# Attention with a relative bias, then routed experts: score products on 64 rows, two groups a visit, earlier transposes, a shorter way to the bias table

## The chip, the cores and the metric

The kernel runs on one core of a Trainium2 chip. The metric is the device time of the kernel in microseconds (us), lower is better. Before the change it is 409.79 us, the median of three runs (408.8 to 410.69).

A core has five engines that work side by side and meet at semaphores: TensorE (PE, matmul; PEld is its weight load), VectorE (DVE), ScalarE (ACT), GpSimd (POOL) and SyncE (SP, which here only starts transfers). An engine carries out its own instructions in order.

## The reference

```
scores = q @ k^T / sqrt(64)                      # 8 batches, 8 heads, 576 positions, head width 64
bias   = bias_table[bucket(|i - j|)]             # 32 buckets; one bucket for all |i - j| >= 128
attn   = exp(scores + bias) / sum                # softmax over the keys
x      = attn @ v                                # 4608 tokens x 512
e      = hash(token_id) mod 8                    # one expert for each token
out    = relu(x @ w1[e]) @ w2[e]                 # 512 -> 1024 -> 512
```

Inputs and output are float32; both kernels multiply in float16 and add up in float32.

## The kernel before

**Stages.** The first stage is the attention; it leaves its rows in DRAM, each at a place in the list of its expert (`xperm`). The second stage takes the experts one after the other: 640 places each, two layers, and a scatter into the output. Its code is the same in both kernels.

**Pairs and groups.** Attention goes over 32 pairs: a batch and two neighbouring heads. A pair has 512 positions in four key tiles of 128, and 64 positions left over (the rest). It is worked in five groups, 0 to 3 for the key tiles and 4 for the rest. A group is a PSUM slot of 128 keys x 2 heads x 512 queries. There are three such slots (`ps`, two banks each), taken in turn.

**One group.** `products(n, g)` multiplies keys by queries; `scores(n, g)` adds the bias by multiplying a flipped identity with a strip of the bias table (`bias`, so a matmul of 384 columns a head), and then ACT takes the exponential of the whole slot into `att`. The bias lies only near the diagonal; the far value is taken off beforehand, since the softmax is blind to a constant. `behind(n, g)` follows with nine of the 45 steps of AV (attention times values, `av_steps`), which runs seven groups behind the scores. A pair's AV fills two accumulators: `aux0` (27 steps) and `aux1` (18 steps). DVE empties them with a reciprocal and a product.

**Both heads in one product.** The keys of a pair lie as 128 rows, 64 of each head. In `kz` each head's 64 rows stand beside 64 rows of zeros, so that a matmul over 128 rows gives the scores of one head; a group has two such matmuls of 512 columns.

**Transposes.** `transpose_qk(n + 1)`, eight matmuls into `pqk`, is placed behind the AV steps of group 3 of pair n. `pqk` shares a bank with `aux1`. DVE then copies `pqk` to `kz` (two copies of 64 rows) and to `qt` (one). The products of pair n+1 come one group later.

**The rest.** Once a batch, `transpose_rest` and `rest_rest` prepare the scores among the 64 leftover positions of all four pairs; `rest_rest` puts them into `prr`, which shares a bank with `aux0`, and ACT takes their exponential into `rr`.

**Order.** The order in each engine is that in which the code is written. `pair_start(n)` puts the loads of pair n+4 on SP's queue and the casts of pair n+2 to float16 on POOL; in some pairs also fills, dispatches (indirect writes of finished rows) and expert weights. A transfer started by SP or ACT may have to wait for an earlier one that used the same completion semaphore.

**The start.** A one-hot matrix (`ohsb`, 32 x 1152) times the table gives the bias for every distance; ACT writes it to DRAM (`t_f`), from where shifted strips are read back: `btb` for the key tiles (heads 0 and 1 first, the other six later) and `btr` for the rest. All of these transfers stand on ACT's queue.

Of the kernel before, what the change touches and what calls it, by code (L numbers as in the profile page):

```python
# [11 lines left out]
F32 = mybir.dt.float32  # L12
F16 = mybir.dt.float16
I32 = mybir.dt.int32
AF = mybir.ActivationFunctionType
# [16 lines left out]
def kernel(  # L32
# [20 lines left out]
    P = 128  # L53
# [19 lines left out]
    GL = 3 * P  # L73
    OH_np = np.zeros((NB, 3, GL), dtype=np.float32)
    for dl in range(3):
        for y in range(GL):
            r = 2 * (y - GL // 2 + 1) + dl - 1
            OH_np[bucket[min(abs(r), S - 1)], dl, y] += 1.0
            OH_np[last, dl, y] -= 1.0
    OH_np = OH_np.reshape(NB, 3 * GL)  # L80
    I128_np = np.zeros((P, 3, P), dtype=np.float16)
# [67 lines left out]
    with tc.tile_pool(name="at", bufs=1) as at, tc.tile_pool(  # L149
# [11 lines left out]
        x_all = at.tile([P, B, NIT, XW], F16, name="x_all")  # L161
        kz = [at.tile([P, 2, KT * P], F16, name=f"kz{i}") for i in range(3)]
        va = [at.tile([P, 2 * KT, VP], F16, name=f"va{i}") for i in range(3)]
# [6 lines left out]
        btb = at.tile([P, H, 3, WB], F16, name="btb")  # L170
        btr = at.tile([P, NPAIR, 2, D + RU], F16, name="btr")
        te = at.tile([P, NGT], I32, name="te")
# [194 lines left out]
        def transpose_qk(n, eng=None):  # L367
            pqk = aux(1, [P, 2, KT * P], F16, "pqk")
            for i, src in enumerate((kh, qh)):
                for t in range(KT):  # L370
                    T, c = t // 2, t % 2
                    o = P * t if i == 0 else NT * P * c + P * T
                    nc.tensor.transpose(  # L373
                        out=pqk[:, i, o : o + P],
                        in_=src[n][:, t, :, :].rearrange("p h d -> p (h d)"),
                        identity=ident[:, :],
                    )
            for hh in range(2):
# [4 lines left out]
            kts[n] = kz[n % 3]  # L383
            qt = at.tile([P, KT * P], F16, name="qt", bufs=2)
            nc.vector.tensor_copy(out=qt[:, :], in_=pqk[:, 1, :])  # L385
            qts[n] = qt
# [31 lines left out]
        def rest_rest(b):  # L418
            prr = aux(0, [P, NPAIR, RC], F32, "prr")
            for m in range(NPAIR):  # L420
                nc.tensor.matmul(
                    out=prr[:, m, :], lhsT=kzr[b % 2][:, m, :],
                    rhs=qtr[b % 2][:, m, :], start=(m == 0), stop=True,
                    skip_group_check=True,
                )
            bias(
                prr[:, :, :].rearrange("p m (o u) -> p m o u", o=2),
                btr[:, :, :, D : D + RU], 2,
            )
# [15 lines left out]
        def products(n, g):  # L445
# [6 lines left out]
            for t in tiles:  # L452
                for hh in range(2):
                    lhsT = kt[:, hh, P * t : P * t + P]
                    rhs = qt[:, :] if g < KT else qtr[b % 2][:, m, :]
                    o = 0 if g < KT else RC * t
                    nc.tensor.matmul(  # L457
                        out=ps[:, hh, o : o + rhs.shape[1]], lhsT=lhsT,
                        rhs=rhs, start=(g < KT or t == 0), stop=True,
                        skip_group_check=True,  # L460
                    )

        def scores(n, g):
# [3 lines left out]
            for hh in range(2):  # L467
# [16 lines left out]
                for t in range(KT - 2, KT):  # L484
# [5 lines left out]
                    )  # L490
                bias(ps[:, hh, 512 - D :], btr[:, m, hh, :D], 2)
            nc.scalar.activation(  # L492
# [79 lines left out]
        nc.scalar.dma_start(out=tbl[:, :], in_=bias_table)  # L572
        ohsb = at.tile([NB, 3 * GL], F32, name="ohsb")
        nc.scalar.dma_start(out=ohsb[:, :], in_=OH_d.ap())
# [3 lines left out]

        def z_init(i):
            nc.gpsimd.memset(kz[i][D:P, 0, :], 0.0)  # L580
            nc.gpsimd.memset(kz[i][:D, 1, :], 0.0)

        z_init(0)
        cast_qk(0, nc.vector, nc.vector)
        bps = [slot("bps") for _ in range(2)]
        ebsb = at.tile([H, 3, GL], F16, name="ebsb")
        for i in range(3):
            nc.tensor.matmul(
                out=bps[i // 2][:H, i % 2, :GL], lhsT=tbl[:, :],
                rhs=ohsb[:, GL * i : GL * i + GL],  # L590
            )
        for i in range(2):
            w = 2 - i
            nc.scalar.activation(
                out=ebsb[:, 2 * i : 2 * i + w, :],
                in_=bps[i][:H, :w, :GL], func=AF.Copy, bias=0.0,
                scale=1.0 / scale,
            )
        nc.scalar.dma_start(
# [3 lines left out]

        def load_band(h0, h1):
            nc.scalar.dma_start(
                out=btb[:, h0:h1, :, :].rearrange("p h a w -> p (h a) w"),
# [5 lines left out]

        load_band(0, 2)
        for hh in range(2):
            for c in range(2):
                for o in range(2):
                    r0 = D * hh + RU * c
                    nc.scalar.dma_start(
                        out=btr[r0 : r0 + RU, :, o, :],
                        in_=bass.AP(  # L620
                            F_d.ap().tensor,
                            (3 * hh + o - c + 1) * GL + P - RU,
                            [[1, RU], [6 * GL, NPAIR], [1, D + RU]],
                        ),
                    )
        transpose_qk(0)
        load(0, "v")
        load(1, "qk")
        for i in range(2):
# [10 lines left out]
        for i in range(3):  # L640
            nc.gpsimd.memset(va[i][:, :, D : D + 1], 1.0)
        cast_v(0)
        load_rest(0, "v")
        load(1, "v")
        cast_qk(1)
        z_init(1)
        cast_vrest(0)
        load_band(2, H)
        load(2)
        load(3)  # L650
        z_init(2)
        nc.sync.dma_start(out=msk[:, :], in_=MSK_d.ap())
# [31 lines left out]
        def pair_start(n):  # L684
# [30 lines left out]
        def behind(n, g):  # L715
# [242 lines left out]
```

## Time and profile before

| | us |
|---|---|
| median of three runs | 409.79 |
| the profiled execution, device time | 408.63 |
| its span, first to last instruction | 406.7 |
| busy: PE, ACT, POOL, DVE | 351.2, 211.4, 167.1, 136.2 |
| ACT exponentials of the scores (160) | 161.7 |
| PE products of key tiles (256) | 78.9 |
| PE bias matmuls of key tiles (256) | 64.6 |
| PE AV matmuls of 65 columns (1280) | 64.6 |

Between the span and the device time lie 1.9 us. Busy times of PE are no sums of work: a matmul counts from its first column to its modelled end, and the next one starts before that end. What a matmul costs PE is read from one start to the next. In the rows, `x8` after a form is the number of instructions in a merged row, and a bracket at the end names the idle time before it and what ended it.

### The profile page before, as it was taken

How to read it: one execution, taken by the hardware profiler on the slowest of the kernel's cores; microseconds unless marked ns; L12 is line 12 of the kernel's file. 1: busy time of each engine (PE TensorE's matmuls, PEld its weight loads, DVE VectorE, ACT ScalarE, POOL GpSimd, SP SyncE). 2: the span in 40 equal slices, each digit the busy share in tenths (PEclk: the TensorE clock that was granted, in tenths of full speed). 3: DMA queues.
4: the chain of work that ended last, by engine and by line, in shares of the span. 5: the costliest groups of instructions: out<-in, count | busy, mean ns of one | idle time of the engine just before them, and what ended most of it. 6: DMA issues, size and time to landing. Idle time of an engine off the chain costs nothing.

```text
span 406.7 us, 9256 instructions
## 1 busy us (share of the span) xinstructions
PE 351.2 (86%) x3792; PEld 229.0 (56%) x3792; DVE 136.2 (33%) x339; ACT 211.4 (52%) x235; POOL 167.1 (41%) x248
## 2 busy tenths in 40 slices
PE   4278999899999999999999807999999999999990
PEld 1035666566666666666666605665657575656650
DVE  1211346544434444344443401323140413223220
ACT  2046877687787877878778601322415051423320
POOL 3713225242576666583846040152333515151331
PEclk9998999999999999999999966999999999999997
DMA  6795967969685755997984025399999999995211
GB/s 172 192 244 147 266 134 215 272 189 269 196 237 169 206 176 134 249 186 212 235 174 94 10 77 175 53 204 159 258 161 266 201 193 261 160 264 115 89 70 61
DMA packets 95107, 72.66 MB, mean 179 GB/s; under 512 B 16295, under 2 KB 86183, under 8 KB 95056
## 3 DMA queue, kind: packets, MB, share of 16 engines
q0 software_dynamic: 17664, 30.96, 36.1%
q1 hardware_dynamic: 72880, 38.98, 35.1%
q10 hardware_dynamic: 4512, 2.04, 2.0%
q8 instruction: 32, 0.52, 0.5%
q14 instruction: 19, 0.16, 0.1%
HBM read 69.27 MB, written 21.03 MB: 222 GB/s over the span
## 4 chain that ended last, share of the span: by engine, by line
PE 71%; DVE 10%; DMA 8%; ACT 4%; issue 2%; SPq 2%; POOL 1%; POOLq 0%; ACTq 0%; DVEq 0%
PE hps L788 17%; PE ops L806 17%; PE ps L457 13%; PE ps L438 9%; PE px L523 8%; DVE kz L379 6%; ACT att L492 3%; PE pqk L373 3%; DVE qt L385 3%; PE xps L767 2%; DMA btb<-t_f 2%; DMA qf<-in_q_dram 2%; DMA xpn<-t_xperm 1%; DMA btr<-t_f 1%; SPq L188 1%
## 5 line engine op out<-in xcount | busy, mean ns | idle before, releaser
L492 ACT ACTIVATE att<-ps 128x1024 f16<-128x1024 f32 x160 | 161.7, 1023 | 58.6 <-PE ps L438 41.8
L794 ACT ACTIVATE h<-hps 128x640 f16<-128x640 f32 x64 | 45.0, 704 | 112.9 <-PE hps L788 112.9
L457 PE MATMUL ps<-qt,kz 128*128 128x512 f16 x256 | 78.9, 391 | 15.4 <-DVE qt L385 13.9
L438 PE MATMUL ps<-btb,idents 128*128 128x384 f16 (+1 forms) x384 | 78.2, 288 | 8.8 <-DMA btb<-t_f 8.8
L806 PE MATMUL ops<-w2t,h 128*128 128x512 f16 x320 | 72.7, 379 | 0.0
L788 PE MATMUL hps<-xpt,w1t 128*128 128x320 f16 x512 | 72.1, 301 | 0.1
L523 PEld LDWEIGHTS <-att 128*128 128x128 f16 x1408 | 61.0, 98 | 18.6 <-ACT rr L430 3.5
L523 PE MATMUL px<-va,att 128*128 128x65 f16 x1280 | 64.6, 193 | 1.2 <-DVE rcp L532 0.4
L438 PEld LDWEIGHTS <-idents 128*128 128x128 f16 x456 | 39.7, 100 | 42.0 <-issue 12.4
L814 POOL DMA_INDIRECT out_dram<-ok,xpn x40 | 39.2, 980 | 57.4 <-DVE ok L813 51.3
L788 PEld LDWEIGHTS <-w1t 128*128 128x128 f16 x512 | 50.4, 99 | 21.2 <-issue 0.3
L379 DVE COPY kz<-pqk 64x512 f16<-64x512 f16 x64 | 27.0, 422 | 77.6 <-PE pqk L373 76.6
L806 PEld LDWEIGHTS <-h 128*128 128x128 f16 x320 | 30.8, 98 | 33.4
L548 POOL DMA_INDIRECT t_xperm<-x_all,ds x40 | 39.4, 985 | 21.9 <-DVE rcp L532 11.3
L813 DVE COPY ok<-ops 128x512 f32<-128x512 f32 x40 | 27.7, 692 | 47.0 <-PE ops L806 47.0
L457 PEld LDWEIGHTS <-kz 128*128 128x128 f16 x512 | 28.2, 99 | 22.2 <-DVE qt L385 18.7
L771 DVE COPY xpt<-xps 128x640 f16<-128x640 f16 x32 | 15.0, 488 | 74.2 <-PE xps L767 59.7
L226 POOL CAST qh<-qf 128x512 f16<-128x512 f32 x31 | 19.0, 613 | 42.9 <-PE pqk L373 25.5
L533 DVE TENSOR_TENSOR x_all<-px,rcp 128x384 f16<-128x384 f32 x64 | 31.4, 491 | 2.2
L234 POOL CAST va<-vf 128x512 f16<-128x512 f32 x32 | 20.0, 624 | 28.5 <-PE px L523 15.7
L132 POOL DMA_DIRECT2D w1t<-in_moe_w_dram x8 | 6.5, 810 | 52.0 <-PE xps L767 51.9
L532 DVE RECIPROCAL rcp<-px 128x6 f32<-128x6 f32 x64 | 11.7, 183 | 42.4 <-PE px L523 42.4
(72 smaller groups left out, 243.0 us busy)
## 6 DMA issues: line engine op xcount, KB each, us to landing
kf<-in_k_dram SPq DMA_DIRECT2D x64, 128.0 KB
qf<-in_q_dram SPq DMA_DIRECT2D x64, 128.0 KB
vf<-in_v_dram SPq DMA_DIRECT2D x64, 128.0 KB
w1t<-in_moe_w_dram POOLq DMA_DIRECT2D x8, 1024.0 KB, 9.6
w2t<-in_moe_w_dram POOLq DMA_DIRECT2D x8, 1024.0 KB, 10.4
t_xperm<-zx SPq DMA_DIRECT2D x10, 514.0 KB
xpn<-t_xperm SPq DMA_DIRECT2D x8, 642.5 KB
btb<-t_f ACTq DMA_DIRECT2D x1, 1152.0 KB
```

The lines of the kernel that those rows point to most:

```text
L379: nc.vector.tensor_copy(out=kz[n % 3][D * hh : D * hh + D, hh, :], in_=pqk[D * hh : D * hh + D, 0, :],)
L438: nc.tensor.matmul(out=out, lhsT=idents[:, which, :], rhs=rhs, start=False, stop=True, skip_group_check=True,)
L457: nc.tensor.matmul(out=ps[:, hh, o : o + rhs.shape[1]], lhsT=lhsT, rhs=rhs, start=(g < KT or t == 0), stop=True, skip_group_check=True,)
L492: nc.scalar.activation(out=att[:, g, :, :], in_=ps[:, :, :], func=AF.Exp, bias=0.0, scale=scale,)
L523: nc.tensor.matmul(out=po, lhsT=lhsT, rhs=rhs, start=(i == 0), stop=(i == len(todo) - 1), skip_group_check=True,)
L533: nc.vector.tensor_tensor(out=x_all[:, b, its[0] : its[0] + ni, :DM].rearrange("p t (m h d) -> p t m h d", h=2, m=NPAIR)[:, :, m, :, :], i ...
L548: sc_in = nc.gpsimd.indirect_dma_start(out=xperm_d.ap()[:, :], out_offset=bass.IndirectOffsetOnAxis(ap=ds2[:, B * t + b : B * t + b + 1], ...
L788: nc.tensor.matmul(out=hps[:, nr, :NR], lhsT=w1h[:, kt, ts(ft, P)], rhs=xt[e][:, kt, ts(nr, NR)], start=(kt == 0), stop=(kt == NPT - 1),)
L794: nc.scalar.activation(out=h1[:, ft, :].rearrange("p (r n) -> p r n", r=NRC), in_=hps[:, :, :NR], func=AF.Relu, bias=0.0, scale=1.0,)
L806: nc.tensor.matmul(out=ops[:, :], lhsT=h1[:, ft, ts(kc, P)], rhs=w2h[:, ft, :], start=(ft == 0), stop=(ft == NFT - 1),)
L813: nc.vector.tensor_copy(out=ok[:, :], in_=ops[:, :])
L814: so = nc.gpsimd.indirect_dma_start(out=out[:, :], out_offset=bass.IndirectOffsetOnAxis(ap=xn[e][:, kc, DM:XW].bitcast(I32), axis=0), in_= ...
```

## The change

1. `kz` with its zeros goes. The keys of both heads are copied to one tile `kt` in a single copy of 128 rows. A product takes 64 rows of `kt` and the same 64 rows of `qt`: one head on the upper half of PE's rows, the other on the lower, into different banks.
2. The loop takes two groups a visit: the products of both, the scores of both, then `early` and then the AV steps of both. With five groups a pair, every fifth visit holds the last group of one pair and the first of the next.
3. `transpose_qk(n + 2)` stands in `early`, behind the scores of the visit with group 3 of pair n and ahead of its AV. The casts on POOL move from n+2 to n+3; the loads stay at n+4. `kt` and `qt` have three buffers.
4. At the start, the one-hot matrix holds only the 129 distances that differ from zero: one float32 matmul (387 columns) for three (384 each), one ACT instruction for two. `btr` comes in four transfers for eight, with longer rows, and `btr` and all of `btb` but heads 0 and 1 move to SP's queue; there they stand ahead of later loads.

```
-            for hh in range(2):
-                nc.vector.tensor_copy(
-                    out=kz[n % 3][D * hh : D * hh + D, hh, :],
-                    in_=pqk[D * hh : D * hh + D, 0, :],
-                )
+            kt = at.tile([P, KT * P], F16, name="kt", bufs=3)
+            nc.vector.tensor_copy(out=kt[:, :], in_=pqk[:, 0, :])
...
-                    lhsT = kt[:, hh, P * t : P * t + P]
-                    rhs = qt[:, :] if g < KT else qtr[b % 2][:, m, :]
+                    r0 = D * hh
+                    rows = slice(r0, r0 + D)
+                    lhsT = kt[rows, P * t : P * t + P]
+                    rhs = (qt[rows, :] if g < KT
+                           else qtr[b % 2][rows, m, :])
...
-        bps = [slot("bps") for _ in range(2)]
-        for i in range(3):
-            nc.tensor.matmul(
-                out=bps[i // 2][:H, i % 2, :GL], lhsT=tbl[:, :],
-                rhs=ohsb[:, GL * i : GL * i + GL],
-            )
+        bps = slot("bps")
+        nc.tensor.matmul(
+            out=bps[:H, 0, : 3 * GN], lhsT=tbl[:, :], rhs=ohsb[:, :],
+        )
...
-        load_band(0, 2)
+        load_band(0, 2, nc.scalar)
+        load(0, "v")
+        load(1, "qk")
...
+        load_band(2, 4, nc.sync)
         load_rest(0, "v")
         load(1, "v")
-        load_band(2, H)
         load(2)
+        load_band(4, H, nc.sync)
+        cast_qk(2)
         load(3)
...
-            if n + 2 < NP:
-                cast_qk(n + 2)
+            if n + 3 < NP:
+                cast_qk(n + 3)
...
-            if g == 3 and n + 1 < NP:
-                transpose_qk(n + 1)
-
-        for n in range(NP):
-            pair_start(n)
-            for g in range(NIT):
+
+        def early(n, g):
+            if (n, g) == (0, 1):
+                transpose_qk(1)
+            if g == 3 and n + 2 < NP:
+                transpose_qk(n + 2)
+
+        order = [(n, g) for n in range(NP) for g in range(NIT)]
+        for i in range(0, len(order), 2):
+            both = order[i : i + 2]
+            for n, g in both:
+                if g == 0:
+                    pair_start(n)
                 products(n, g)
+            for n, g in both:
                 scores(n, g)
+            for n, g in both:
+                early(n, g)
+            for n, g in both:
                 behind(n, g)
```

PE before, in the middle of pair 3: the end of group 1 with `rest_rest`, then the AV steps that end `aux1`, then group 2 (`kz_75` holds the keys, `kzr_84` and `qtr_86` the rest of the next batch; what stands in brackets is waited for).

```order
L421 LDWEIGHTS kzr_84 [waits DVE_49]
L421 MATMUL prr<-qtr_86,kzr_84 128x64 [waits PE_49]
...
L438 MATMUL prr<-btr,idents 128x256
...
L523 MATMUL px<-vt_81,rr_87 128x130
L457 LDWEIGHTS kz_75
L457 MATMUL ps<-qt,kz_75 128x512 [waits Activation_49]
...
L438 MATMUL ps<-btb,idents 128x2x192
L523 LDWEIGHTS att [waits Activation_49]
L523 MATMUL px<-va_80,att 128x65 [waits Pool_49]
```

PE after the change at the same place (`kzr_81` and `qtr_83` are the rest of the next batch).

```order
L461 MATMUL ps<-qt,kt 128x512 [waits Activation_49]
...
L439 MATMUL ps<-btb,idents 128x2x192
L421 LDWEIGHTS kzr_81 [waits DVE_49]
L421 MATMUL prr<-qtr_83,kzr_81 128x64 [waits PE_49]
...
L439 MATMUL prr<-btr,idents 128x4x32
...
L527 MATMUL px<-vt_78,rr_84 128x130
L527 LDWEIGHTS att [waits Activation_49]
L527 MATMUL px<-va_77,att 128x65
```

Before, the products and scores of group 2 stand between `rest_rest` and the AV steps that wait for ACT to have emptied `prr`. After, they stand ahead of `rest_rest`, and nothing but nine AV steps lies between it and that wait; ACT has both groups' exponentials in its queue ahead of `rr`.

SP's queue at the start, before:

```order
L188 DMA qf<-in_q_dram 128x2x128 x2
L188 DMA kf<-in_k_dram 128x2x128 x2
L214 DMA vr<-in_v_dram 32x4x64 x4
L188 DMA vf<-in_v_dram 128x2x128 x2
L188 DMA qf<-in_q_dram 128x2x128 x2
L188 DMA kf<-in_k_dram 128x2x128 x2
```

and after:

```order
L191 DMA kf<-in_k_dram 128x2x128 x2
L615 DMA btr<-t_f 32x4x480 x4
L601 DMA btb<-t_f 128x6x256
L217 DMA vr<-in_v_dram 32x4x64 x4
L191 DMA vf<-in_v_dram 128x2x128 x2
L191 DMA qf<-in_q_dram 128x2x128 x2
L191 DMA kf<-in_k_dram 128x2x128 x2
```

Five transfers that read `t_f` now stand between the loads of pair 1's keys and those of pair 2's queries and keys.

## Rows read from the trace of the kernel before

**Rows 1.** Stretches: length; busy us and instructions by engine; granted clock; DMA share; GB/s.

```profile
31.80:231.60 199.80, 185.04 (x2697) 129.71 (x2697) 86.95 (x250) 158.94 (x163) 100.14 (x156) 0.99 0.75 190
231.60:249.60 18.00, 4.32 (x67) 3.85 (x68) 3.02 (x8) 0.00 (x0) 4.87 (x5) 0.66 0.45 144
249.60:406.70 157.10, 147.40 (x972) 89.18 (x969) 41.26 (x69) 45.05 (x64) 49.62 (x52) 0.98 0.75 163
65.00:110.00 45.00, 41.38 (x614) 29.15 (x612) 22.77 (x67) 34.96 (x37) 18.83 (x35) 1.00 0.84 235
```

**Rows 2.** Timeline of PE: one pair in mid-attention, its five groups.

```profile
110.58 0.60 PE L457 MATMUL ps<-qt,kz 128*128 128x512 f16 x2 [0.43 <-DVE qt L385]
111.03 0.49 PE L438 MATMUL ps<-btb,idents 128*128 128x384 f16 x2
111.35 0.44 PE L523 MATMUL px<-va,att 128*128 128x65 f16 x9
111.62 0.59 PE L457 MATMUL ps<-qt,kz 128*128 128x512 f16 x2
...
114.76 0.39 PE L373 MATMUL pqk<-idents,kh 128*128 128x128 f16 x4
...
115.21 0.40 PE L457 MATMUL ps<-qtr,kz 128*128 128x64 f16 x8
115.44 0.27 PE L479 MATMUL ps<-qt,kzr 128*128 128x256 f16 x1
...
115.83 0.35 PE L523 MATMUL px<-va,att 128*128 128x65 f16 x6
...
116.78 0.60 PE L457 MATMUL ps<-qt,kz 128*128 128x512 f16 x2 [0.43 <-DVE qt L385]
```

**Rows 3.** Waits: engine, line, waited for; us in total, times, longest.

```profile
PE ps L457 <- DVE qt L385: 13.9, 31, 1.0
POOL qrh L246 <- DMA qr<-in_q_dram: 14.8, 4, 6.2
```

**Rows 4.** Timeline of ACT and PE: exponentials back to back; `rr` and who waits.

```profile
111.61 4.10 ACT L492 ACTIVATE att<-ps 128x1024 f16<-128x1024 f32 x4 [0.75 <-PE ps L438]
124.31 1.99 ACT L492 ACTIVATE att<-ps 128x1024 f16<-128x1024 f32 x2 [0.75 <-PE ps L438]
126.20 0.38 ACT L430 ACTIVATE rr<-prr 128x256 f16<-128x256 f32 x1
126.63 0.33 PEld L523 LDWEIGHTS <-att 128*128 128x128 f16 x9 [0.47 <-ACT rr L430]
```

**Rows 5.** Groups by form of L457: x count, busy us, mean ns, idle before.

```profile
L457 PE MATMUL ps<-qt,kz 128*128 128x512 f16 x256 | 78.9, 391 | 15.4 <-DVE qt L385 13.9 <-ACT att L492 1.6
L457 PEld LDWEIGHTS <-kz 128*128 128x128 f16 x512 | 28.2, 99 | 22.2 <-DVE qt L385 18.7 <-issue 2.8 <-POOL kh L226 0.5
```

**Rows 6.** The table's matmuls (ns; first and last start), and the load behind them.

```profile
L588 PE MATMUL bps<-ohsb,tbl x6: 794/842/842, 4.5 to 7.6; 32*8 32x384 f32 x6
...
8.38 0.34 PEld L373 LDWEIGHTS <-kh 128*128 128x128 f16 x4 [1.28 <-issue]
```

**Rows 7.** Timeline of the start, all engines and queues.

```profile
4.46 3.99 PE L588 MATMUL bps<-ohsb,tbl 32*8 32x384 f32 x6 [4.46 <-DMA ohsb<-t_bias_oh]
...
8.45 2.43 SPq L214 DMA_DIRECT2D vr<-in_v_dram  x4
8.49 0.48 ACT L594 ACTIVATE ebsb<-bps 8x384 f16<-8x384 f32 x1 [0.48 <-PE bps L588]
...
10.92 0.50 ACTq L599 DMA_DIRECT2D t_f<-ebsb  x1
...
13.24 0.45 ACTq L605 DMA_DIRECT2D btb<-t_f  x1
13.35 0.99 SPq L188 DMA_DIRECT2D kf<-in_k_dram  x2
...
19.61 0.61 POOL L226 CAST kh<-kf 128x512 f16<-128x512 f32 x1 [1.30 <-DMA kf<-in_k_dram]
...
23.59 0.38 ACTq L605 DMA_DIRECT2D btb<-t_f  x1
...
31.80 0.48 PE L438 MATMUL ps<-btb,idents 128*128 128x384 f16 x2 [2.11 <-DMA btb<-t_f]
```

**Rows 8.** DMA issues of the page: count, KB each.

```profile
kf<-in_k_dram SPq DMA_DIRECT2D x64, 128.0 KB
t_xperm<-zx SPq DMA_DIRECT2D x10, 514.0 KB
```

More of the change, by code (lines that the diff above doesn't have):

```diff
@@ L73 @@
     GL = 3 * P
-    OH_np = np.zeros((NB, 3, GL), dtype=np.float32)
+    GN = MAXD + 1
+    OH_np = np.zeros((NB, 3, GN), dtype=np.float32)
     for dl in range(3):
-        for y in range(GL):
-            r = 2 * (y - GL // 2 + 1) + dl - 1
+        for y in range(GN):
+            r = 2 * y - MAXD + dl - 1
             OH_np[bucket[min(abs(r), S - 1)], dl, y] += 1.0
             OH_np[last, dl, y] -= 1.0
-    OH_np = OH_np.reshape(NB, 3 * GL)
+    OH_np = OH_np.reshape(NB, 3 * GN)
     I128_np = np.zeros((P, 3, P), dtype=np.float16)
@@ L170 @@
         btb = at.tile([P, H, 3, WB], F16, name="btb")
-        btr = at.tile([P, NPAIR, 2, D + RU], F16, name="btr")
+        btr = at.tile([P, NPAIR, GL + D + RU], F16, name="btr")
+        bro = [
+            btr[:, :, GL * o : GL * o + D + RU] for o in range(2)
+        ]
         te = at.tile([P, NGT], I32, name="te")
@@ L425, in rest_rest @@
                 )
-            bias(
-                prr[:, :, :].rearrange("p m (o u) -> p m o u", o=2),
-                btr[:, :, :, D : D + RU], 2,
-            )
+            for o in range(2):
+                bias(
+                    prr[:, :, RU * o : RU * o + RU],
+                    bro[o][:, :, D : D + RU], 2,
+                )
             nc.scalar.activation(
@@ L490, in scores @@
                     )
-                bias(ps[:, hh, 512 - D :], btr[:, m, hh, :D], 2)
+                bias(ps[:, hh, 512 - D :], bro[hh][:, m, :D], 2)
             nc.scalar.activation(
@@ L572 @@
         nc.scalar.dma_start(out=tbl[:, :], in_=bias_table)
-        ohsb = at.tile([NB, 3 * GL], F32, name="ohsb")
+        ohsb = at.tile([NB, 3 * GN], F32, name="ohsb")
+        ebsb = at.tile([H, 3, GL], F16, name="ebsb")
+        nc.gpsimd.memset(ebsb[:, :, :], 0.0)
         nc.scalar.dma_start(out=ohsb[:, :], in_=OH_d.ap())
@@ L577 @@
         load_rest(0, "kq")
[L579 to L583, printed above, removed]
         cast_qk(0, nc.vector, nc.vector)
-        bps = [slot("bps") for _ in range(2)]
-        ebsb = at.tile([H, 3, GL], F16, name="ebsb")
-        for i in range(3):
-            nc.tensor.matmul(
-                out=bps[i // 2][:H, i % 2, :GL], lhsT=tbl[:, :],
-                rhs=ohsb[:, GL * i : GL * i + GL],
[L591 to L598, printed above, removed]
+        bps = slot("bps")
+        nc.tensor.matmul(
+            out=bps[:H, 0, : 3 * GN], lhsT=tbl[:, :], rhs=ohsb[:, :],
+        )
+        nc.scalar.activation(
+            out=ebsb[:, :, P - 1 : P - 1 + GN],
+            in_=bps[:H, 0, : 3 * GN].rearrange("h (a b) -> h a b", a=3),
+            func=AF.Copy, bias=0.0, scale=1.0 / scale,
+        )
         nc.scalar.dma_start(
@@ L611, in load_band @@
             )
-        load_band(0, 2)
+        load_band(0, 2, nc.scalar)
+        load(0, "v")
+        load(1, "qk")
         for hh in range(2):
             for c in range(2):
[L616 to L625, printed above, removed]
+                r0 = D * hh + RU * c
+                nc.sync.dma_start(
+                    out=btr[r0 : r0 + RU, :, :],
+                    in_=bass.AP(
+                        F_d.ap().tensor, (3 * hh + 1 - c) * GL + P - RU,
+                        [[1, RU], [6 * GL, NPAIR], [1, GL + D + RU]],
+                    ),
+                )
         transpose_qk(0)
-        load(0, "v")
-        load(1, "qk")
         for i in range(2):
```

13 lines of the change are left out of this document (5 added, 8 removed).

## The prediction

> **What bounds the kernel now.** Read the stretches first. Behind 249.6 us lies the expert stage, 157.1 us, and ahead of it 18.0 us of dispatch and first loads; the change touches neither, so both stay [rows 1]. Of the rest, the first 31.8 us are the start, up to the bias of pair 1, and 199.8 us hold pairs 1 to 31. In these PE is busy for 185.0 us and ACT for 158.9 [rows 1]: PE sets the pace, but ACT is near enough to be the next bound.
>
> Then one pair on PE, read from start to start [rows 2]. From 110.58 to 116.78 it takes 6.20 us. The two products of a group take 0.45 (110.58 to 111.03; 0.44 in the others), its two bias matmuls 0.32, nine AV steps 0.27. The transposes take 0.45, the eight small products of group 4 0.23, its bias part 0.39, and its AV, with three steps of double width, some 0.35. Then PE stands for 116.78 - 115.83 - 0.35 = 0.60, of which the trace books 0.43 as a wait for `qt` (the other 0.17 is the last matmul running out). Four groups of 1.03, the last one, transposes and wait make 6.14; the missing 0.06 are wide AV steps in other groups. The wait comes 31 times [rows 3], once a pair. Without it a pair is 5.60.
>
> ACT's own pace: four exponentials back to back take 4.10 us, 1.025 each [rows 4], so 5.13 a pair. No change on PE brings a pair below that.
>
> **Part 1: products on 64 rows.** No row of before shows two matmuls side by side. The bounds: the second head's product costs nothing beside the first (0.22 a group in place of 0.44), or they still follow each other (0.44). I take 0.22: they share neither rows of the array nor a bank. Four groups save 0.88; the small products save between nothing and 0.12, I take 0.06. A pair is then 4.66 on PE.
>
> The Trainium skill, "TensorE: Matmul & The Clock Gate", section on the measured speedup against the span model, says that matmuls on different row groups overlap with a few ns between their starts. By that rule the lower bound holds; no run here shows it so far.
>
> The change from 128-row matmuls to 64-row ones and back, twice a visit and so five times a pair, is new. The nearest row is the one change of tile in this trace, from the table's 32-row matmuls to the transposes [rows 6]. A pass of these takes 3.99 us / 6 = 0.64 from start to start less the last one's tail: six starts from 4.46 to 7.6 are 0.63 apart [rows 6, 7]. So the last one, started at 7.6, had taken its columns in at 8.24, and the next weight load starts at 8.38: a gap of 0.14, though that load had been free to go ahead since 7.1 (idle 1.28). The bounds are 0 (the gap may have another cause, a late transfer) and 0.27: a product takes 391 ns from start to end against 0.22 of columns, so 0.17 of running out, and a weight load of 99 ns that can't run ahead [rows 5]. I take 0.14, the one row that shows such a step. Five of them cost 0.70: a pair is 5.36 on PE.
>
> The Trainium skill, "TensorEngine Tiling (Array Packing)", section "Key Properties", says that changing the tiling mode drains the engine, while changing the tile within a mode does not. This speaks against the change; by a drain that shows the whole run-out and the load, the sum would be the third rival's below. The gap of 0.14 agrees with a drain but is shorter than that.
>
> **Part 2: two groups a visit, three slots.** A plain visit is now 2 x (0.22 + 0.32 + 0.27) + 2 x 0.14 = 1.90 on PE, ACT's two exponentials 2.05: ACT leads there. The second product of a visit waits for the slot of the visit before's first group. From the end of that exponential on: 0.05 to PE (126.58 to 126.63 [rows 4]), product 0.22, switch 0.14, bias 0.32, and 0.26 from there to ACT's start (111.35 [rows 2] to 111.61 [rows 4]), in all 0.99. ACT is meanwhile busy for 1.025 with the second group, so three slots just do. A visit with transposes is 1.90 + 0.45 = 2.35, 0.30 over ACT's 2.05, and 0.03 of slack takes little of it. One such visit comes in each pair, so a pair is 5.13 + 0.27 = 5.40. Against 6.20, 31 pairs save 31 x 0.80 = 24.8 us. The wait for `qt` is in that; what is late next is ACT.
>
> **What two groups a visit cost: `rr`.** Eight times `rest_rest` fills `prr`, and `aux0` is free again only when ACT has made `rr`. Before, a group's products and bias lie in between, and still PE waits 0.47 [rows 4]. After, ACT has both exponentials ahead of `rr`: from the start of the first to the end of `rr` it needs 126.58 - 124.31 = 2.27 [rows 4]. Counted from the end of the first group's bias, `rr` is there after 0.26 + 2.27 + 0.05 = 2.58. PE gets there after the second bias 0.32, `rest_rest` about 0.25 (an estimate from rows 2: four small matmuls are half of 0.23, one of 256 columns about 0.11) and nine AV steps 0.33: 0.90. It waits 1.68, or 1.21 more than before, and behind it wait the next visit's products, so ACT runs dry as well. Eight times: +9.7 us.
>
> **Part 3: earlier transposes.** No instruction is added. DVE makes two copies for three. The transposes of pair 2 now fall in pair 0, which makes them part of the start.
>
> **Part 4: the start.** The table's matmul loses four of six passes (2.6 us) and ACT one instruction (0.48) [rows 7]. `ebsb` is then written near 6 in place of 8.97. `t_f` went out at 10.92, 1.95 later; it had to wait for a transfer. I let it go between 7 and 8.5, and 2.3 later (10.92 to 13.24) it has landed. That isn't what ends the start, though. PE takes its instructions in order, and ahead of pair 1's bias there now stand the transposes of pair 2. Before, the keys of pair 2 go out until 14.34 and are cast at 19.61, when they have landed, 5.3 later [rows 7]. After, SP stands at the `btr` transfers until `t_f` has landed, at 9.3 to 10.8 (before, the next one went at 8.45), then issues five transfers more, some 2.5: the keys go out until 17.7 to 19.2, land at 23 to 24.5 and are cast by 24.5. Transposes, group 4 and a product need 1.2 more: pair 1's bias starts near 25.8, against 31.80, which waited for the late `btb` that ACT could only send at 23.59 [rows 7]. That saves 6.0. The bounds: 10, if SP isn't held up and the loads land as before; 3, if the longer `btr` rows (some 490 KB for 196) slow the loads.
>
> **Sum**, against the profiled execution, 408.63 us (1.2 below the median of 409.79): 408.63 - 24.8 + 9.7 - 6.0 = 387.5.
>
> **The rivals.**
> - *The switch is free.* PE 4.66 a pair, the transposing visit 2.07; ACT's pace, 5.15, holds: 31 x 1.05 = 32.6; 408.63 - 32.6 + 9.7 - 6 = 379.7. For: the gap of 0.14 may be a transfer. Against: that load had nothing else to wait for that I can see.
> - *Loads come late.* Pairs 2 to 11 move six loads of 128 KB and a fill of 514 KB [rows 8], with the rest some 1.4 MB a pair. The queue moved 235 GB/s at a share of 0.84, so 280 at most [rows 1]: 5.0 of 5.4 us. The casts come a pair closer to their loads, and POOL already waited up to 6.2 us for a batch's rest [rows 3]. If this stops PE for 1.3 us in each of 7 batches: 396.5. Against: PE never waited for a cast in mid-attention.
> - *The wide switch*, 0.27: a pair is 4.66 + 1.35 = 6.01; 31 x 0.19 = 5.9; 408.63 - 5.9 + 9.7 - 6 = 406.4, hardly a change.
> - *Slower: the heads don't run side by side.* Then the change doesn't do what it says. A pair is 5.60 + 0.70 = 6.30, 0.10 more than before: 408.63 + 3.1 + 9.7 - 6 = 415.4. It decides from the point where a pair with its switches is above 6.08. For: no row shows the overlap. Against: the halves touch different rows and banks.
>
> **How the numbers follow.** Mine 0.48, free switch 0.20, late loads 0.14, wide switch 0.09, no overlap 0.09. About 0.5% is what can be told from no change here (406.6 to 410.7 against the profiled execution). Faster: mine, free switch, late loads and a little of the wide switch, 0.84; same 0.07, most of the wide switch; slower 0.09, no overlap. The range takes in the free switch with a start that saves 10 (375.7) and the wide switch: 375 to 408. Mine alone, with the bounds of the start: 383 to 391.
>
> **What would show it.** Right: starts of two heads' products a few ns apart and a bias 0.22 + 0.14 behind; no wait for `qt`; ACT idle only near transposes; a wait for `rr` of about 1.7 us eight times; pair 1's bias near 26. Wrong: a product pair of 0.44; a gap of 0.27 or none at each switch; waits of PE for casts; SP's loads landing after 28 at the start; a longer stretch ahead of the experts than 18 us.

## The result, and the profile after

The changed kernel takes 391.81 us (median of 4 runs, 391.13 to 392.61), the kernel before 409.58 us on the same chip: a ratio of 0.9565, 95% interval 0.9536 to 0.9595. The forecast was 387.5, with a range of 375 to 408. The profiled execution of after took 392.0 us, its span 390.2.

First the stretches of after, cut at the same events as [rows 1]: pair 1's bias, the last attention product, the first expert product. The columns are those of [rows 1].

```profile
23.97:214.80 190.83, 169.99 (x2699) 117.05 (x2696) 72.09 (x217) 152.48 (x164) 101.98 (x159) 0.99 0.80 209
214.80:232.20 17.40, 4.28 (x67) 3.88 (x68) 3.07 (x8) 0.04 (x1) 4.86 (x5) 0.70 0.46 148
232.20:390.20 158.00, 148.18 (x972) 89.58 (x970) 41.25 (x69) 45.06 (x64) 49.59 (x52) 0.98 0.75 162
```

The start ends 7.8 us earlier (31.80 to 23.97), pairs 1 to 31 take 9.0 less (199.80 to 190.83), and dispatch and experts together 0.3 more. PE lost 15.1 us of busy time in the pairs (185.04 to 169.99), but the stretch shrank by 9.0 only: 6 us of it came back as standing.

Now PE in 7 us of mid-attention, against [rows 2]. Columns: start, duration, engine, line, operation, count, and the idle time before it with its releaser. The new names: `kt` is a pair's transposed keys, both heads in one buffer of 128 rows; `qt` and `qtr` are read by 64 rows.

```profile
95.21 0.45 PE L527 MATMUL px<-va,att 128*128 128x65 f16 x9 [1.43 <-ACT rr L431]
95.59 0.39 PE L461 MATMUL ps<-qt,kt 64*128 64x512 f16 x2
95.82 0.28 PE L461 MATMUL ps<-qtr,kt 64*128 64x64 f16 x8
...
97.66 0.33 PE L527 MATMUL px<-vt,att 128*128 128x130 f16 x3
97.92 0.61 PE L461 MATMUL ps<-qt,kt 64*128 64x512 f16 x4
98.46 0.82 PE L439 MATMUL ps<-btb,idents 128*128 128x384 f16 x4
...
102.20 0.29 PE L461 MATMUL ps<-qtr,kt 64*128 64x64 f16 x8
102.33 0.38 PE L461 MATMUL ps<-qt,kt 64*128 64x512 f16 x2
```

Two products (x2) last 0.38 to 0.39 from the first start to the last end, as long as one of them alone (391 ns in [rows 5]); before they took 0.60 [rows 2]. So the heads run beside each other. The next operation starts 0.23 after the first (95.59 to 95.82), where it was 0.44 to 0.45. Four products and the change of tile behind them take 98.46 - 97.92 = 0.54; at 0.22 to 0.23 for two products, 0.08 to 0.10 is left for the change. Ahead of them stand three AV steps of 130 columns, which take 0.26 to the first product (97.66 to 97.92); by the 0.03 of a step of 65 columns (nine take 0.27 [rows 2]) the steps alone are some 0.17, so the change into the smaller tile is about 0.09. The eight small ones take 0.13 (102.20 to 102.33) for 0.23.

The waits of after, against [rows 3]; columns: engine, line, waited for, then us in total, times, longest.

```profile
PE px L527 <- ACT rr L431: 11.4, 8, 1.4
PE pr L392 <- POOL krh L249: 6.5, 3, 3.3
POOL qh L229 <- DMA qf<-in_q_dram: 23.3, 12, 4.6
POOL qrh L249 <- DMA qr<-in_q_dram: 12.4, 5, 5.9
```

PE's 31 waits for `qt` are gone. The eight for `rr` are here, 1.43 each. Two rows are new in kind: PE waits for a cast of POOL (`krh`, the keys of a batch's rest), and POOL for pairs' queries 23.3 us.

Then ACT, against [rows 4].

```profile
103.46 5.71 ACT L496 ACTIVATE att<-ps 128x1024 f16<-128x1024 f32 x6 [0.53 <-PE ps L439]
109.72 3.99 ACT L496 ACTIVATE att<-ps 128x1024 f16<-128x1024 f32 x4 [0.55 <-PE ps L439]
114.12 3.87 ACT L496 ACTIVATE att<-ps 128x1024 f16<-128x1024 f32 x4 [0.41 <-PE ps L439]
117.88 0.39 ACT L431 ACTIVATE rr<-prr 128x256 f16<-128x256 f32 x1
119.69 1.02 ACT L496 ACTIVATE att<-ps 128x1024 f16<-128x1024 f32 x1 [1.41 <-PE ps L439]
```

Six exponentials take 5.71, 0.95 each: that is ACT's pace. The four of [rows 4], 1.025 each, came no faster because PE's groups came 1.03 apart [rows 2].

`rr` is made once a batch of four pairs, always at the same place in the work, and so marks the batches. Its starts, in us:

| kernel | pair 1 | pair 3 | 7 | 11 | 15 | 19 | 23 | 27 |
|---|---|---|---|---|---|---|---|---|
| before | 34.40 | 48.33 | 75.03 | 100.62 | 126.20 | 151.77 | 177.34 | 202.92 |
| after | 28.50 | 45.86 | 71.86 | 94.76 | 117.88 | 140.79 | 163.70 | 189.21 |

Before, five batches take 25.57 to 25.59. After, four take 22.90 to 23.12, some 2.62 less each. But 45.86 to 71.86 took 26.00 (before 26.70) and 163.70 to 189.21 took 25.51 (before 25.58), and 23.97 to 45.86, from pair 1's bias on, 21.89 (before 16.53). These three are called disturbed here, the four alike ones undisturbed.

Four stretches of after by engine (columns as in [rows 1]): a disturbed batch, two undisturbed ones, and the other disturbed one.

```profile
46.00:72.00 26.00, 22.14 (x352) 15.28 (x352) 12.31 (x37) 19.55 (x22) 9.46 (x19) 1.00 0.78 205
72.00:95.00 23.00, 21.48 (x350) 15.04 (x350) 10.31 (x33) 19.64 (x22) 8.74 (x17) 1.00 0.84 252
95.00:118.00 23.00, 21.64 (x350) 15.03 (x350) 9.05 (x27) 19.43 (x22) 13.29 (x21) 1.00 0.75 218
164.00:189.00 25.00, 21.65 (x350) 15.01 (x350) 9.05 (x27) 19.03 (x21) 11.97 (x18) 1.00 0.88 181
```

PE's work is the same in the last two (21.6), at the same granted clock; the 2 us between them are standing. Where PE stands shows in its own rows; in these stretches they are, beside `rr`, the waits of 0.8 us and more:

```profile
36.53 0.28 PE L392 MATMUL pr<-idents,krh 128*128 128x128 f16 x2 [3.26 <-POOL krh L249]
...
61.94 0.28 PE L392 MATMUL pr<-idents,krh 128*128 128x128 f16 x2 [0.83 <-POOL krh L249]
...
66.17 0.30 PE L309 MATMUL rps<-oh,cnt 128*128 128x320 f16 x1 [1.40 <-DVE oh L299]
...
181.38 0.28 PE L392 MATMUL pr<-idents,krh 128*128 128x128 f16 x2 [2.43 <-POOL krh L249]
```

0.83 + 1.40 and 2.43 are the size of what the two batches lack; the 1.40 is a wait for DVE's routing work (`oh`), not for a load. POOL's rows of the third one show why `krh` is late: each cast waits for its load, and they come one behind the other, since POOL takes them in order.

```profile
177.07 0.61 POOL L229 CAST qh<-qf 128x512 f16<-128x512 f32 x1 [4.50 <-DMA qf<-in_q_dram]
177.91 0.61 POOL L229 CAST kh<-kf 128x512 f16<-128x512 f32 x1 [0.23 <-DMA kf<-in_k_dram]
178.99 0.40 POOL L249 CAST qrh<-qr 128x256 f16<-128x256 f32 x1 [0.47 <-DMA qr<-in_q_dram]
180.92 0.40 POOL L249 CAST krh<-kr 128x256 f16<-128x256 f32 x1 [1.53 <-DMA kr<-in_k_dram]
```

In the stretch from 24 to 46 the wait of 3.26 is half of what is lost. (That stretch also holds 2.4 us of PE's waits for `rr`, nearly two of them, where its 2.25 pairs would have 0.8 by share.) Behind it the granted clock falls, and the four bias matmuls of a visit take 1.46 for 0.82 (a window, then PE's rows):

```profile
36.50:40.00 3.50, 3.47 (x29) 2.02 (x30) 1.38 (x5) 1.18 (x2) 2.22 (x5) 0.63 0.86 232
```

```profile
32.18 0.82 PE L439 MATMUL ps<-btb,idents 128*128 128x384 f16 x4
...
37.97 1.46 PE L439 MATMUL ps<-btb,idents 128*128 128x384 f16 x4
```

Where the loads come from: SP's queue in 46 to 72. The 40 transfers that it starts there take 24.4 us to issue, in a stretch of 26.

```profile
46.33 1.33 SPq L191 DMA_DIRECT2D qf<-in_q_dram  x2
...
50.03 5.05 SPq L274 DMA_DIRECT2D te<-in_moe_token_ids_dram  x6
...
61.16 0.94 SPq L191 DMA_DIRECT2D qf<-in_q_dram  x2
```

Six small transfers of the routing table `te` hold the queue for 5.05 us, the rest's loads follow, and the next pair's queries leave at 61.16, 14.8 us after the last ones. The other disturbed batch is of another kind: in 164 to 189 SP starts only 26 transfers, and an issue takes 0.80 us there on average, where the median of all loads of q, k and v is 0.47. In that stretch POOL's queue also loads expert weights, and the DMA share is 0.88 at 181 GB/s; 72 to 95 moved 252 GB/s at 0.84 and lost nothing.

### The profile page after: what moved, and what is told of

Read it like the earlier page. It is cut to its first block, busy times and chain, and to the rows that moved or that the text cites. A ratio compares the mean times of both kernels' runs of the same rounds, so it can differ in the third digit from the quotient of the medians.

```text
span 390.2 us, 9219 instructions
## 1 busy us (share of the span) xinstructions
PE 333.6 (85%) x3796; PEld 215.6 (55%) x3796; DVE 120.8 (31%) x307; ACT 203.2 (52%) x234; POOL 165.2 (42%) x243
## 4 chain that ended last, share of the span: by engine, by line
PE 58%; DMA 16%; SPq 10%; POOL 5%; issue 4%; ACT 3%; DVE 1%; POOLq 0%; DVEq 0%; ACTq 0%
PE hps L793 18%; PE ops L811 18%; PE ps L439 6%; PE px L527 5%; DMA vf<-in_v_dram 5%; SPq L191 5%; PE ps L461 5%; ACT att L496 3%; PE xps L772 3%; DMA qf<-in_q_dram 3%; PE pqk L376 2%; POOL t_xperm L552 2%; SPq L205 2%; SPq L217 2%; DMA btb<-t_f 1%
## 5 line engine op out<-in xcount | busy, mean ns | idle before, releaser
L496 ACT ACTIVATE att<-ps 128x1024 f16<-128x1024 f32 x160 | 154.2, 1021 | 51.5 <-PE ps L439 50.6
L439 PE MATMUL ps<-btb,idents 128*128 128x384 f16 (+1 forms) x384 | 68.8, 293 | 3.3 <-DMA btb<-t_f 3.3
L527 PE MATMUL px<-va,att 128*128 128x65 f16 x1280 | 57.9, 194 | 11.8 <-ACT rr L431 11.4
L527 PEld LDWEIGHTS <-att 128*128 128x128 f16 x1408 | 55.4, 98 | 18.4 <-ACT rr L431 11.2
L439 PEld LDWEIGHTS <-idents 128*128 128x128 f16 x464 | 32.5, 99 | 29.8 <-issue 21.3
L461 PE MATMUL ps<-qt,kt 64*128 64x512 f16 x256 | 44.5, 397 | 0.3 <-DVE rnk L319 0.2
L229 POOL CAST qh<-qf 128x512 f16<-128x512 f32 x31 | 19.1, 616 | 35.3 <-DMA qf<-in_q_dram 23.3
L382 DVE COPY kt<-pqk 128x512 f16<-128x512 f16 x32 | 13.6, 424 | 64.9 <-PE pqk L376 64.9
L537 DVE TENSOR_TENSOR x_all<-px,rcp 128x384 f16<-128x384 f32 x64 | 31.4, 491 | 2.2
L772 PE MATMUL xps<-idents,xpn 128*128 128x128 f16 x160 | 13.9, 230 | 13.1 <-DMA xpn<-t_xperm 12.9
```

Source lines behind the costliest of these rows:

```text
L439: nc.tensor.matmul(out=out, lhsT=idents[:, which, :], rhs=rhs, start=False, stop=True, skip_group_check=True,)
L461: nc.tensor.matmul(out=ps[:, hh, o : o + rhs.shape[1]], lhsT=lhsT, rhs=rhs, start=(g < KT or t == 0), stop=True, skip_group_check=True,)
L496: nc.scalar.activation(out=att[:, g, :, :], in_=ps[:, :, :], func=AF.Exp, bias=0.0, scale=scale,)
L527: nc.tensor.matmul(out=po, lhsT=lhsT, rhs=rhs, start=(i == 0), stop=(i == len(todo) - 1), skip_group_check=True,)
L537: nc.vector.tensor_tensor(out=x_all[:, b, its[0] : its[0] + ni, :DM].rearrange("p t (m h d) -> p t m h d", h=2, m=NPAIR)[:, :, m, :, :], i ...
L772: nc.tensor.transpose(out=xps[:, ts(sc, P)], in_=xpn[:, sc, ts(kt, P)], identity=ident[:, :],)
```

## The experiments

The theory: the tiling, two groups a visit and the early transposes each do their part; what the time lacks is lost to loads. Rivals: the change of tile eats what the products save; the loss is `rr`; the early transposes do it all. Runs of one group shared a chip and a reference; chips differ, so undisturbed batches are compared across groups before times are.

**First group** (before: 414.05 us). Products over all 128 rows again; `rest_rest` between the products and the scores of a visit; the loads of a batch's rest a pair earlier; the start of before.

```
e1  -  lhsT = kt[rows, P*t : P*t+P];  rhs = qt[rows, :] or qtr[..][rows, m, :]
    +  lhsT = kt[:, P*t : P*t+P];     rhs = qt[:, :]    or qtr[..][:, m, :]
```

> Each product takes all 128 rows again (both heads' rows at once, so a score is the sum of two heads and the output is not the reference's); order, visits, start and transposes stay. The two heads run side by side and a switch of the tile costs about 0.095 us (theory): a group's products go from about 0.22 to 0.43 us, the gaps at the switches (0.09 in, 0.10 out) go, a pair on TensorE grows by 0.88 + 0.10 - 0.48 = 0.50 us, 31 pairs by 15, less a few us that TensorE waits for ScalarE today: 402 to 407 us. Rival, the switch eats the whole gain of the side-by-side products: 390 to 394 us.

Measured: 408.49 us, 0.9868 (0.9817 to 0.9918). PE in e1:

```profile
76.91 1.03 PE L461 MATMUL ps<-qt,kt 128*128 128x512 f16 x4
77.78 0.81 PE L439 MATMUL ps<-btb,idents 128*128 128x384 f16 x4
```

Four products take 0.87 to the bias, with no change of tile, for 0.54 with it (97.92 to 98.46 above): 0.33 less a full visit, before the change back. Undisturbed batches take 24.42 (73.73 to 98.15 and 177.78 to 202.20), 1.5 more than the 22.9 of after and of e3 beside it. So with two groups a visit the change of tile does not eat the gain: that rival falls.

```
e2  in behind():  -  if n == 1: rest_rest(0) ;  if m == 3 and b + 1 < B: rest_rest(b + 1)
    between products and scores:  +  the same two, at g == 1
```

> rest_rest stands between the products and the scores of its visit, so ScalarE makes rr ahead of both groups' exponentials. Theory: the eight waits of TensorE for rr (1.43 us each in the trace, some 1.6 from column to column) go, and ScalarE no longer runs dry behind them: 11 to 13 us less, 379 to 381 us. Rival, ScalarE sets the pace there and the wait costs TensorE nothing that ScalarE would not cost anyway: 388 to 392 us, with new waits for exponentials in the place of those for rr.

Measured: 397.48 us, 0.9572 (0.9529 to 0.9614). PE's waits for `rr` are gone and an undisturbed batch is 21.5 (71.67 to 93.21), 1.4 less, the size of the wait. Of the time less is left: waits for `krh` rose from 6.5 to 13.7 us in all:

```profile
PE pr L392 <- POOL krh L249: 13.7, 4, 6.6
```

At 37.70, in PE's own rows, the longest of them:

```profile
37.70 0.39 PE L392 MATMUL pr<-idents,krh 128*128 128x128 f16 x2 [6.61 <-POOL krh L249]
```

`rr`'s wait costs what the trace books, but taking it away brings PE sooner to a load. How much time was gained is not shown, since after did not run on this chip. The ratio is that of after on the first chip (0.9565); but e4, which ran here at 0.9759 and on a chip where after has 0.9676 at 0.9774 (e4b below), suggests that after would be nearer 0.967 here, and e2 some 4 us better (an estimate from these ratios).

```
e3  pair_start:  +  if n == 0: load_rest(1) ;  if m == 3 and b + 2 < B: load_rest(b + 2)   (ahead of load(n + 4))
                 -  if b + 1 < B and m == 0: load_rest(b + 1)
```

> The loads of a batch's rest go out one pair earlier and ahead of that pair's other loads. Theory: the three waits of TensorE for the casts of the rest (3.3, 0.8 and 2.4 us, 6.5 in all) go, and POOL is held up less behind them: 4 to 7 us less, 385 to 388 us. Rival, the transfers as a whole are the limit, so the wait only passes to the casts of queries and keys: 390 to 393 us, with waits of TensorE for kh or qh.

Measured: 402.96 us, 0.9728 (0.9675 to 0.9782): not better, by either ratio of after (0.9565, and 0.9676 below). PE still waits 3.27 us for `krh` near 38 us, since POOL makes that cast behind a pair's cast that waits 6.13 us for its load, and POOL's waits for pairs' queries rise from 23.3 (after) to 40.4 us. Moved up in one queue, a load pushes the others back.

```
e4  the table's three matmuls, the eight btr transfers, and btb and btr on ACT's queue as before; all else as after
```

> The start of the kernel before (three float32 matmuls, eight transfers for btr, all of btb and btr on ScalarE's queue), everything else as after. Theory: pair 1's bias comes near 31 to 33 us again in place of 24.0, but the loads of batch 1's rest are no longer late (3.3 us of TensorE's wait, in pair 2, go), so part of it was given back: 395 to 398 us. Rival, all of it counts: 399 to 401 us. Other rival, all of it was given back by the late loads: 391 to 393 us.

Measured: 404.67 us, 0.9759 (0.9712 to 0.9806). Its first `rr` comes at 34.43, where before has 34.40 and after 28.50. What that is worth at the end needs after on the same chip: the third group.

**Second group** (before: 409.19 us). One group a visit; the kernel before with the transposes in front of AV and two pairs ahead, and nothing else; e2 and e3 together.

```
e5  -  for i in range(0, len(order), 2): both = order[i : i + 2]
    +  for i in range(0, len(order), 1): both = order[i : i + 1]
```

> One group a visit, 64-row products and all else as after. 160 visits for 80. Theory, a switch costs about 0.095 us: 160 switches more, 15 us, less what the waits for rr get shorter (products and scores of a group lie in between again, some 1 us eight times): 396 to 400 us. Rival, the switches are hidden behind waits for ScalarE: 383 to 388 us.

Measured: 393.31 us, 0.9625 (0.9577 to 0.9672). An undisturbed batch takes 23.49, 0.5 more than in after: twice the changes of tile, while the weight loads' waits for `rr` are only 2.8 us in all in place of 11.2. Two groups a visit gain a little, net.

```
e6  (from before)  qt: bufs=2 -> 3;  cast_qk(n + 2) -> cast_qk(n + 3);  transpose_qk(n + 1) in behind() -> transpose_qk(n + 2) ahead of it
```

> The kernel before with one part of the change: queries and keys transposed two pairs ahead and in front of AV. Theory: the wait for qt (0.60 us from column to column, 31 times) goes, nothing takes its place: 18 us less than before, 390 to 393 us, about as much as the whole change. Rival, ScalarE's exponentials become late instead (their own pace is 5 of 6.2 us a pair, so only in part): 396 to 402 us.

Measured: 397.07 us, 0.9698 (0.9671 to 0.9725). Its stretch of one undisturbed batch:

```profile
120.85:144.00 23.15, 23.07 (x351) 16.70 (x349) 11.11 (x32) 20.51 (x22) 16.28 (x26) 1.00 0.69 200
```

PE stands for 0.08 of 23.15: the batch loses 2.42 us, 0.60 a pair, which is the standing for `qt` counted out of [rows 2]. So the largest part of the gain in the batches needs neither tiling nor two groups. With one group a visit the tiling even loses: 23.49 (e5) against 23.15. The rows show where: a group of 512 columns takes 1.03 in both, from its products to the next group's (122.27 to 123.30 in e5, 124.02 to 125.05 in e6), so the two changes of tile take all that its products save; group 4, with small products, takes 1.07 (121.20 to 122.27) against 0.98 (123.04 to 124.02). With two groups a visit the tiling wins: without it 24.42 (e1), with it 22.96, each with the wait of 1.43 for `rr`. So after is 0.2 better than e6, and 1.6 where `rr` is out of the way (21.5 in e2). All these are from different chips; after's undisturbed batch takes 22.90 on a1's chip too (72.42 to 95.32).

```
e7  e2 and e3
```

> Both edits of e2 and e3 on top of the change: rr ahead of the exponentials, loads of the rest a pair earlier. Theory, the two losses are separate: 16 to 19 us less than after, 373 to 376 us. Rival, a faster TensorE only meets the loads sooner (they are near their limit in pairs 2 to 11 and at the expert weights): 379 to 383 us, with waits for casts.

Measured: 393.61 us, 0.96 (0.9565 to 0.9635). Undisturbed 21.46; disturbed 27.5 (44.87 to 72.33), 26.5 (93.80 to 120.33) and 30.3 (163.26 to 193.57). PE's waits are now split over two casts:

```profile
PE pqk L376 <- POOL kh L229: 8.3, 3, 5.7
PE pr L392 <- POOL krh L249: 8.3, 2, 4.9
```

What is gained in one batch is waited for in another.

**Third group** (before: 412.97 us). After once more; the old start; loads five pairs ahead in place of four (with e2); and that with e3 and with POOL's casts of the rest and the dispatches ahead of a pair's cast.

```
a1  after, unchanged
e4b e4, unchanged
e9  e2, and  load(n + 4) -> load(n + 5), bufs=4 -> 5, load(4) at n == 0
e13 e9 and e3, and  cast_qk(n + 3) moved behind cast_rest, cast_vrest and the dispatches
```

> The changed kernel itself, unchanged, so that the three others of this call have it on their own chip: 0.954 to 0.960 of before if the ratio holds from chip to chip. Rival: the four kernels of the first call ran on a chip where before itself takes 1.1% longer (414.1 us), and where the changed kernel's ratio may be another; then this ratio says how far their distances from 391.8 us may be read.

> The start of the kernel before, everything else as after, now beside the changed kernel on one chip. Theory, the start is worth what pair 1's bias shows (31.8 to 24.0) less the waits for the rest of batch 1 that it brings (3.3 us): 4 to 6 us slower than the changed kernel. Rival, all of it counts: 7 to 9 us slower. Other rival, all given back: within 1.5 us.

Measured: after 399.24 us, 0.9676 (0.9622 to 0.9729); e4b 405.08, 0.9774 (0.971 to 0.9838). The old start costs 4.0 us by the ratios and 5.8 between the medians, about as forecast, but the two intervals overlap a little, so that this size is not clear of the noise. On this chip after gains less than on the first, which is taken up below.

> rr ahead of the exponentials as in e2, and the loads of a pair go out one pair earlier (n+5, five buffers), so that the casts have the lead over the loads that they had before the change. Theory A, the lead is what is missing: POOL's waits for qf (11 of more than 1.5 us in e2) mostly go, with them the long waits of TensorE for krh and the falls of its clock: 376 to 382 us. Theory B, the transfers' rate is the limit: the waits move but stay, 388 to 392 us.

Measured: 399.06 us, 0.9661 (0.9622 to 0.9699), as after on this chip. POOL's waits for pairs' queries fall to 7.5 us, but one late load of the rest takes their place:

```profile
PE pr L392 <- POOL krh L249: 11.7, 2, 7.8
```

> e9 and besides the loads of the rest ahead of a pair's other loads and one pair earlier, and POOL's casts of the rest and its dispatches ahead of the casts of queries and keys in a pair's start, so that a late load of queries holds up no other cast. Theory A (POOL's order and lead): undisturbed batches of 21.5 us all along, 373 to 378 us, waits for krh gone. Theory B (the rate of the transfers): 386 to 392 us, with waits for kh or qh in place of krh.

Measured: 406.32 us, 0.9847 (0.9813 to 0.9882), 7 us worse than after. A dispatch that waits for its fill now holds the next pair's casts behind it on POOL, and PE waits for these:

```profile
POOL t_xperm L552 <- DMA qf<-in_q_dram: 12.3, 1, 12.3
...
PE pqk L376 <- POOL kh L229: 8.2, 4, 4.5
```

(The profile puts the wait down to `qf`, which is not an operand of `t_xperm`. That it was the last fill, which SP sent at 103.84, is argued from the code; its landing is not shown.)

**Fourth run** (before: 408.33 us): e13 with the dispatches behind a pair's cast again, so that only the casts of the rest's queries and keys go ahead.

```
e14 order on POOL:  cast_rest;  cast_qk(n + 3);  cast_vrest;  dispatches
```

> rr ahead of the exponentials, loads of a pair one pair earlier (five buffers), loads of the rest a pair earlier and ahead of the pair's others, casts of the rest ahead of those of queries and keys; the dispatches stay behind them (in e13 the first dispatch, which waits for the last fill, held up the casts for 12.3 us). Theory A, what is late is a matter of lead and of POOL's order: waits for krh and kh under 3 us in all, 0.93 to 0.945 of before. Theory B, what SP's queue and the transfers can bring is the limit in the batches with the routing loads, the fills and the expert weights: undisturbed batches of 21.5 us but the same disturbed ones, 0.955 to 0.967 of before.

Measured: 388.65 us, 0.9544 (0.9501 to 0.9587). The interval overlaps that of after (0.9536 to 0.9595), so it isn't shown to be better. Undisturbed batches take 21.5 to 21.9, but 39.65 to 74.37 takes 34.7 and 160.97 to 187.51 takes 26.5. Its stretches show where:

```profile
40.00:74.00 34.00, 24.37 (x349) 16.75 (x348) 11.88 (x36) 19.14 (x21) 10.96 (x22) 0.80 0.79 218
75.00:95.00 20.00, 19.99 (x339) 14.21 (x336) 10.71 (x33) 17.98 (x20) 8.56 (x16) 1.00 0.87 254
161.00:187.00 26.00, 22.60 (x344) 15.33 (x342) 9.15 (x27) 19.46 (x21) 16.69 (x26) 0.93 0.88 195
```

In 75 to 95 PE never stands. Over the whole run PE waits 1.2 us for `krh` and 6.8 for `kh`, so that these waits passed from one cast to the other rather than went. In the first stretch it stands for 9.6 of 34 us, nearly all at one place:

```profile
65.63 0.58 PE L376 MATMUL pqk<-idents,kh 128*128 128x128 f16 x4 [8.54 <-DVE x_all L537]
```

`x_all` (L537) reads the accumulator whose bank the transposes are to fill. It is late because DVE takes its work in order, and stood at the routing table (DVE's rows):

```profile
63.71 0.18 DVE L286 TENSOR_SCALAR te<-te 128x40 int32<-128x40 int32 x1 [9.16 <-DMA te<-in_moe_token_ids_dram]
...
65.06 0.42 DVE L537 TENSOR_TENSOR x_all<-px,rcp 128x256 f16<-128x256 f32 x1
```

That table comes late by SP's order (SP's row of e14):

```profile
58.39 3.90 SPq L274 DMA_DIRECT2D te<-in_moe_token_ids_dram  x6
```

In after the same transfers leave at 50.03 and DVE does not stand there. e14's own edits put the loads of one more pair and of one more rest ahead of them, and `te` went back by 8.4 us, while PE reached this work some 6 us sooner (`rr` of pair 3 at 39.65 for 45.86). DVE's wait for `te` shows in the four runs whose loads of the rest go earlier, and only there: 1.87 us in e3, 2.61 in e7, 8.39 in e13, 9.16 in e14, with `te` sent at 55.65, 56.00, 58.76 and 58.39.

So e2, e7, e9 and e14 each took away one wait and met the next load: `krh`, then `kh`, then `te`. That a longer lead or another order on POOL alone would set the time free was not borne out in e9, e13 and e14. But e14's longest wait was made by its own order on SP's queue, and an order that keeps `te` ahead of the added loads was not run; without that wait of 8.5 us e14 might have been clearly better than after. That SP's issues and the transfers don't keep up agrees with all of the runs and is not proven by them. Which of the two it is was not told apart: no run moved transfers to another queue or took bytes away. The rows of after lean to the issues in 46 to 72 (40 transfers at 0.78 of the DMA share) and to the transfers in 164 to 189 (26 slow issues beside the expert weights at 0.88).

## Why the prediction was right, step by step

The pieces, by the same reckoning as in the prediction, against the 387.5:

- **Products on 64 rows.** 0.22 a group was forecast, 0.23 measured; the small ones save 0.10, forecast 0.06. The rivals "no overlap" and, with 0.10, "wide switch" fall.
- **The change of tile.** 0.14 forecast from one gap; 0.08 to 0.10 out, and about 0.09 in, were measured. "Free switch" falls too: what stands against it in the prediction held.
- **ACT as the bound.** Here the mechanism was off. 1.025 an exponential was no pace of ACT's but that of PE's groups in before; ACT goes at 0.95. So in a plain visit ACT does not lead by 0.15, as forecast: its two exponentials take 1.90, and PE takes 1.89 (97.92 to 99.81). An undisturbed batch of before is 4 x 6.20 + 0.78; one of after, 22.96, less the same 0.78 and the longer wait for `rr` (1.43 - 0.47 = 0.96), leaves 5.30 a pair, for 5.40 forecast: -3.1 us over 31 pairs.
- **The wait for `rr`.** 1.68 forecast, 1.43 measured: -2.0 over eight. It moved to the AV behind it, as said, and e2 gives it back in an undisturbed batch.
- **The transposes.** The 31 waits for `qt` went, as forecast, and e6 shows that this alone is 0.60 a pair.
- **The start.** Pair 1's bias was to be at 25.8 and is at 23.97: -1.8. The order of events is that forecast, with the cast of pair 2's keys last. The keys went out until 18.88, as forecast, but landed 2.0 later, not 5.3 (rows of SP, POOL and PE of after):

```profile
17.90 0.98 SPq L191 DMA_DIRECT2D kf<-in_k_dram  x2
...
20.84 0.61 POOL L229 CAST kh<-kf 128x512 f16<-128x512 f32 x1 [0.49 <-DMA kf<-in_k_dram]
...
21.51 0.61 PE L376 MATMUL pqk<-idents,kh 128*128 128x128 f16 x4 [2.33 <-POOL kh L229]
...
23.97 0.83 PE L439 MATMUL ps<-btb,idents 128*128 128x384 f16 x2
```

- **Loads.** This is the step that failed. The prediction gave late loads 0.14 as a case beside its own, on the ground that PE never waited for a cast in mid-attention. It is no case beside the others: it came on top. PE waited three times for `krh`, 6.5 us in all, where before had no such wait for a cast by POOL. At the undisturbed saving of 2.62 a batch the three disturbed stretches would have taken 15.06 (16.53 less 2.25 pairs' share, 1.47), 24.08 and 22.96; they took 6.8, 1.9 and 2.55 more, in all 11.3. The rival's price was 9, its places seven batches of 1.3; the trace shows two batches and the start. Not all of the 11.3 is shown to be loads: 6.5 are the waits for `krh`, 1.4 is DVE's routing work, some 1.6 of the first stretch is `rr` beyond its share, and the remainder, which has the fallen clock in it, was not split. The rival's ceiling of 280 GB/s, taken from one stretch in proportion to its share, was no price either: after moved 252 GB/s at a share of 0.84 in a batch that lost nothing, and 181 at 0.88 in one that lost 2.55 us.

387.5 - 3.1 - 2.0 - 1.8 + 11.3 and 0.3 for dispatch and experts is 392.2; the profiled execution took 392.0. So that the time came out within 5 us was luck: smaller terms, all taken too dear, paid 6.9 of the 11.3 that the sum did not have.

## What to carry to other kernels

When a stage is made faster, work out its transfers at the new pace batch by batch, not for the mean: their number on one queue, and the bytes that other queues move beside them; that the old profile shows no wait for them says only how much slack the old pace left. A pair of matmuls on half the rows saves its columns in full, but each change of tile cost about 0.1 us here, so work of one tile has to be put together before it pays (one group a visit: 23.49 a batch with, 23.15 without). And of a change with several parts, run the cheapest part alone: the early transposes gave 2.42 us a batch, where the whole change gave 2.62. Last, when loads are moved forward in a queue, look at what they push back: `te` went back by 8.4 us.

## What the hardware showed that was not expected

- The ratio of the same two kernels was 0.9565 (0.9536 to 0.9595) on one chip and 0.9676 (0.9622 to 0.9729) on another, whose kernel before took 412.97 us for 409.58. The second lost time in batches that went undisturbed on the first: `rr` to `rr` 25.7 and 27.1 (120.78 to 146.46 to 173.51) where the first has 22.9. In the first of them the granted clock is 1.00 on both chips and PE's busy time much the same (21.95 for 21.48 us), so PE stood longer; part of that is 4.5 us of waits for ACT's exponentials over the whole run, in seven places, which the first chip does not have. Why was not found.
- ACT's exponentials of 128x1024 take 1.02 us each in the records and 0.95 from start to start.
- A late load costs more than its wait. After the stand of 3.26 us the mean granted clock of 36.5 to 40 was 0.63, a mixture of the levels of 2.4 and 1.2 GHz, against 1.00 in the 6.5 us that ended with the stand. In e14 it was 1.00 over 40 to 57, before the stand of 8.54, and 0.50, the lower level, over 65.6 to 74, behind it.
- A wait booked to an engine can be that of an instruction queued ahead on it: 8.54 us of PE "for `x_all`" were DVE's 9.16 for a table.
